# Weight sums for y by seven products: made by GpSimd alone, with longer DMA rows

## The chip, the cores and the metric

One NeuronCore of a Trainium2 chip runs the whole program. The metric is device time in microseconds, the median of several executions; lower is better. Engines in what follows: TensorE (PE), VectorE (DVE), ScalarE (ACT), GpSimd (POOL), and SyncE (SP), whose queue issues all DMAs of this kernel.

## The reference

Windowed attention over 8 x 8 heads of 576 positions with head dimension 64 (half of the heads look at the last 32 positions, half at every fourth of the last 128), and behind it a feed-forward layer with a PReLU over all 4608 tokens.

```
scores = scale * q @ k.T                    # (8, 8, 576, 576), masked to -1e9 outside the window
attn = exp(scores - max); attn = attn / (sum(attn) + 1e-9)
x = (attn @ v) as 4608 x 512
h = x @ w_in                                # w_in 512 x 2048
g = max(h, 0) + alpha * min(h, 0)
out = g @ w_out                             # w_out 2048 x 512
```

All of it in float32; a matrix operand is held as a high and a low float32r part, and a product is three passes (high-high, high-low, low-high).

## The kernel before, in words

The 4608 tokens are nine blocks of 512. Blocks 0 to 2 go through both layers in the plain form. Blocks 3 to 8 are done in pairs (t = 3, 5, 7), in `paired_stage` (L1155 onwards), which fills the span from about 348 us on. A pair (t, t+1) is done in two groups (grp 0, 1) of half the hidden units each. A group has a product stage for h and a stage for y.

- In the product stage h is made by seven matrix products instead of eight, on sums of quarter matrices. A unit of four hidden slices (four units, i = 0 to 3, to a group) takes products 1, 7, 6, 2, 5, 3, 4, each 12 matmuls in two blocks of 6 (`product`, L666); 3 and 4 are done within the next unit. Results lie in PSUM banks A, B, C. VectorE adds bank B or C to a staged copy (`add`, L715), which frees the bank for the next unit; ScalarE and VectorE then make the activation and its high and low parts (L722, L726, L730, L734).
- y of pair 3 is done plainly (`phase_y`, L930): 32 steps of 12 matmuls, in 4 output blocks c. y of pairs 5 and 7 is done by seven products too (`seven_y`, L1050), in 29 steps; there the finished banks are added to a partial sum in SBUF by `put` (L979), which frees them.
- The weights come from DRAM copies (wS for h, wO for y) made earlier, through a ring of ten places (`feed`, L614): each place is filled again when its weights have been used.
- y by seven products needs sums of the four quarters of w_out for each of eight sets i = 0 to 7 (NFP). They go into DRAM copy wY, and the ring reads them from there in pairs 5 and 7. `second_sum` (L1062) makes one set in three parts: `fetch` loads 1 MB of wO in four DMAs with rows of 512 B (L1074); `sums` does one addition of 128x1024 and four of 128x256 on VectorE (L1078, L1081); `parts` makes the high part on ScalarE (L1085) and the low part on VectorE (L1086) and stores both (L1088).
- The last 12 attention head pairs run within these stages: scores (L226, L250), maxima on VectorE (L283, L286), exponentials on ScalarE (L296), divisions and transpose on VectorE (L303 to L311), values (L326, L273). The next pair's k and q are loaded behind the scores, its v behind the values (L200, L201, L208).

Every engine runs its instructions in the order in which the code writes them; nothing reorders them. Work is put between the matmuls by hooks: a table from a step (of y) or a pair (unit, product) of the product stage to operations. `SUMS` (L1059) says at which step of which y stage a set's three parts stand: for (0, 0), that is pair 3 and grp 0, sets 1, 2, 3; for (0, 1) sets 4, 5; for (2, 0), pair 5 and grp 0, sets 6, 7. Set 0 is early: its loads are issued ahead of the first product stage, its `sums` stand in unit 0 behind product 6 and its `parts` behind product 5. Attention hooks of a step stand ahead of those of the sums. In `phase_y` a scoring stands at steps 2, 7, 12, 17, 22 in grp 0 and at 3, 8, 13 in grp 1; values follow eight steps later.

Buffers of the sets: `wy_spare` for set 0, and the ring's neighbours g1 to g4 (`gbuf`), two to a set, which also hold the staged copies of the product stage.

Of the kernel before, what the change touches and what calls it, by code (L numbers as in the profile page):

```python
# [8 lines left out]
F32 = mybir.dt.float32  # L9
F32R = mybir.dt.float32r  # L10
# [5 lines left out]
ALU = mybir.AluOpType  # L16

P = 128
# [7 lines left out]
HB = 9  # L26
# [5 lines left out]
NC = DM // P  # L32
NF = DFF // P
NSTD = 3
NFP = NF // 2
# [3 lines left out]
GP = 4  # L39
# [28 lines left out]
def tile_window_attention_prelu_ffn(  # L68
# [34 lines left out]
    marks = dram.tile([2 * NC, 1], F32, name="marks")  # L103
    wY = dram.tile([NFP, 4, P, 2, 2 * P], F32, name="wY")

# [71 lines left out]
    class Pair:  # L177
# [123 lines left out]
        def divisions(self):  # L301
            self.rs = rs = sml.tile([P, HB], F32, tag="rs", name=f"rs_{self.id}")
            nc.vector.tensor_scalar_add(rs, self.sm, 1e-9)  # L303
            nc.vector.reciprocal(out=rs, in_=rs)
            nc.vector.tensor_tensor(
                out=self.pr, in0=self.pr, in1=rs[:, :, None].broadcast_to([P, HB, BK]), op=ALU.mult)
# [217 lines left out]
    WBLOCK = {1: 0, 2: 1, 4: 2, 3: 3, 7: 4, 5: 5, 6: 6}  # L524
    YBLOCK = {6: 0, 7: 1, 3: 2, 5: 3}

# [50 lines left out]
    for t in range(NSTD, NTILE, 2):  # L577
        for grp in range(NFP // GP):
# [379 lines left out]
    def seven_y(t, grp, us, hooks):  # L958
# [72 lines left out]
        for n, (i, q) in enumerate(YSTEPS):  # L1031
# [11 lines left out]
            else:  # L1043
# [3 lines left out]
                for c in range(2):  # L1047
                    for k, (a, e) in enumerate(PASSES):
                        b = 2 * a + c if q in YBLOCK else 2 * c + a
# [9 lines left out]
    SUMS = {  # L1059
# [3 lines left out]
    }  # L1063

    def second_sum(i, rooms):


        room = {}

        def fetch():  # L1070
            room["x"], room["t"] = rooms()
# [4 lines left out]
        def sums():  # L1076
            x, t = (room[a].rearrange("p o c n -> p (o c n)") for a in "xt")
            nc.vector.tensor_tensor(out=t, in0=x, in1=t, op=ALU.add)  # L1078
            t = t.rearrange("p (q n) -> p q n", q=4)
# [3 lines left out]
        def parts():  # L1083
            x, t = (room[a].rearrange("p o c n -> p (o c n)") for a in "xt")
            nc.scalar.copy(out=x.bitcast(F32R), in_=t)  # L1085
            nc.vector.tensor_tensor(out=t.bitcast(F32R), in0=t, in1=x, op=ALU.subtract)  # L1086
            for a, w in enumerate((x, t)):
# [3 lines left out]
        return fetch, sums, parts  # L1091

    def second_sums(hooks, at):

        for i, *steps, k in SUMS.get(at, ()):
            ops = second_sum(i, lambda i=i, k=k: [gbuf([P, 2, NC, P], F32, f"wy{i}_{a}", k + a) for a in range(2)])
            for n, op in zip(steps, ops):
                hooks.setdefault(n, []).append(op)

# [56 lines left out]
    def paired_stage():  # L1156
# [4 lines left out]
        del cells["xB1"]  # L1161
        spare = const.tile([P, 2, 2, NC, P], F32, tag="xB1", name="wy_spare")
        early = second_sum(0, lambda: [spare[:, a] for a in range(2)])
        early[0]()
        late = []
        for t in range(NSTD, NTILE, 2):
            for grp in range(NFP // GP):
# [21 lines left out]
                if grp and t + 2 < NTILE:  # L1189
# [10 lines left out]
                second_sums(hooks, (t - NSTD, grp))  # L1200
                if seven:
# [49 lines left out]
    nc.vector.memset(pr0, 0.0)  # L1251
    nc.vector.memset(least, TOP_BIAS)
    pairs[0].load_qk()
    nc.sync.dma_start(out=pieces, in_=masks[:, 2 * NMASK:])
# [300 lines left out]
```

## Time and profile before

| | before |
|---|---|
| median of 3 runs | 876.75 us (875.34 to 880.34) |
| profiled execution, its own time | 878.21 us |
| its span | 876.1 us |
| TensorE busy | 839.7 us (96%) |
| VectorE busy | 623.8 us (71%) |
| ScalarE busy | 445.7 us (51%) |
| GpSimd busy | 47.0 us (5%), all of it before 320 us |
| DMA | 182.43 MB, 66.0% of the 16 engines' time |

A busy share is a mean over stages with different limits. What bounds a stretch is read from TensorE's waits there: a row of that view names the waiting engine and its instruction, then the engine and instruction that it waited for. Rows of the timeline carry start, duration, engine, line, operation, and in brackets the idle time ahead of the instruction and what ended it. A DMA row of SPq is the issue of a transfer on SyncE's queue and not the transfer itself.

### The profile page before, as it was taken

The page shows a single profiled execution, that of the slowest core. Times are in us where ns is not written, and L with a number is a line of the kernel's source. Part 1 is how long each engine was busy: PE and PEld are TensorE (multiplying, and loading weights), DVE is VectorE, ACT ScalarE, POOL GpSimd, SP SyncE. Part 2 cuts the span into 40 slices and gives each one's busy share as a digit, 9 for nine tenths or more (in the row PEclk, how much of TensorE's full clock was granted, in tenths as well). Part 3 has the DMA queues.
Part 4 walks back from the last instruction along what each step waited for, and adds up shares of the span by engine and source line. Part 5 has one row for each costly group of instructions (what it writes and reads, how often), then busy time and mean ns, then how long its engine had stood idle before and what let it go on. Part 6 is the DMA issues. An engine that isn't in the chain of part 4 may idle for free.

```text
span 876.1 us, 20220 instructions
## 1 busy us (share of the span) xinstructions
PE 839.7 (96%) x8094; PEld 684.3 (78%) x8094; DVE 623.8 (71%) x1071; ACT 445.7 (51%) x1226; POOL 47.0 (5%) x52
## 2 busy tenths in 40 slices
PE   7789999999999999699989998999899999999998
PEld 5567888888888888488778877888688888888886
DVE  5887766766676778477746787698649988843992
ACT  6785766424434444265435563566356536643650
POOL 0000000200514520000000000000000000000000
PEclk9999999999999999899999999999999999999999
DMA  7743344027899953778866688666965777666674
GB/s 254 255 160 120 137 165 150 28 92 218 276 288 315 301 193 116 253 220 237 283 223 194 172 258 284 213 195 209 327 212 180 203 258 215 193 196 192 194 207 145
DMA packets 134010, 182.43 MB, mean 208 GB/s; under 512 B 10014, under 2 KB 77726, under 8 KB 133918
## 3 DMA queue, kind: packets, MB, share of 16 engines
q1 hardware_dynamic: 133918, 181.15, 66.0%
q8 instruction: 64, 1.05, 0.5%
q14 instruction: 28, 0.23, 0.1%
HBM read 139.17 MB, written 41.94 MB: 207 GB/s over the span
## 4 chain that ended last, share of the span: by engine, by line
PE 83%; DMA 7%; DVE 5%; ACT 2%; SPq 2%; issue 2%; DVEq 0%; ACTq 0%
PE y L501 15%; PE h L453 15%; PE pA L666 14%; PE qA L1050 9%; PE pC L666 7%; PE y L930 6%; PE qC L1050 4%; PE pB L666 4%; PE o L326 3%; DMA q<-qT 2%; PE s L226 2%; PE qB L1050 2%; DMA wy<-wO 1%; DMA wy_spare<-wO 1%; PE s L250 1%
## 5 line engine op out<-in xcount | busy, mean ns | idle before, releaser
L453 PE MATMUL h<-x,w_dt.float32r 128*128 128x512 f32 x576 | 143.5, 399 | 0.9 <-ACT x L380 0.8
L501 PE MATMUL y<-g,w_dt.float32r 128*128 128x512 f32 x576 | 138.3, 389 | 0.0
L453 PEld LDWEIGHTS h<-x,w_dt.float32r 128*128 128x128 f32 x576 | 108.8, 191 | 24.5 <-ACT x L380 0.9
L501 PEld LDWEIGHTS y<-g,w_dt.float32r 128*128 128x128 f32 x576 | 108.0, 188 | 22.5
L296 ACT ACTIVATE pr<-pr,nm 128x64 f32<-128x64 f32 x216 | 72.3, 338 | 63.4 <-DVE nm L286 63.4
L479 ACT CAST g<-m 128x512 fp32r<-128x512 f32 x48 | 29.7, 619 | 74.8 <-DVE m L474 71.8
L666 PE MATMUL pA<-parts_w,ring_w 128*128 128x512 f32 x228 | 56.6, 390 | 0.0
L666 PE MATMUL pA<-parts_w,ring_xA 128*128 128x512 f32 x228 | 56.4, 390 | 0.0
L666 PEld LDWEIGHTS pA<-parts_w,ring_xA 128*128 128x128 f32 x228 | 42.7, 188 | 8.9
L666 PEld LDWEIGHTS pA<-parts_w,ring_w 128*128 128x128 f32 x228 | 42.7, 188 | 8.9
L806 DVE TENSOR_TENSOR gp<-stage,gp 128x512 fp32r<-128x512 f32 x64 | 42.8, 684 | 2.8 <-ACT gp L802 2.8
L484 DVE TENSOR_TENSOR g<-m,g 128x512 fp32r<-128x512 f32 x48 | 33.7, 701 | 15.5 <-ACT g L479 15.4
L1050 PE MATMUL qA<-gp,ring_w 128*128 128x512 f32 x162 | 40.9, 402 | 3.8 <-DVE py L979 3.8
L802 ACT CAST gp<-stage 128x512 fp32r<-128x512 f32 x64 | 37.5, 618 | 7.8 <-DVE stage L799 6.4
L473 DVE TENSOR_SCALAR m<-h,al 128x512 f32<-128x512 f32 x27 | 20.2, 749 | 29.7 <-PE h L453 29.7
L930 PE MATMUL y<-gp,ring_w 128*128 128x512 f32 x168 | 41.0, 396 | 0.0
L296 ACT ACTIVATION_READ_ACCUMULATOR pr<-pr,nm 128x1 f32 x216 | 40.9, 189 | 0.0
L1050 PEld LDWEIGHTS qA<-gp,ring_w 128*128 128x128 f32 x162 | 31.4, 195 | 10.9 <-DVE py L979 4.2
L666 PE MATMUL pC<-parts_w,ring_xA 128*128 128x512 f32 x114 | 29.6, 404 | 8.7 <-DVE stage L715 8.7
L722 ACT ACTIVATE n<-stage 128x512 f32<-128x512 f32 x44 | 27.9, 634 | 19.1 <-DVE stage L715 14.5
L930 PE MATMUL y<-gp,ring_xA 128*128 128x512 f32 x156 | 37.3, 393 | 0.0
L930 PEld LDWEIGHTS y<-gp,ring_w 128*128 128x128 f32 x168 | 31.5, 190 | 6.8
(181 smaller groups left out, 1604.3 us busy)
## 6 DMA issues: line engine op xcount, KB each, us to landing
ring_xA<-wS SPq DMA_DIRECT2D x67, 256.0 KB, 2.9
ring_w<-wS SPq DMA_DIRECT2D x66, 256.0 KB, 3.0
ring_g<-wS SPq DMA_DIRECT2D x35, 256.0 KB, 3.1
ring_w<-wO SPq DMA_DIRECT2D x34, 256.0 KB, 3.1
ring_xA<-wO SPq DMA_DIRECT2D x33, 256.0 KB, 3.0
wO<-w_dt.float32r SPq DMA_DIRECT2D x32, 256.0 KB, 4.5
wS<-wc SPq DMA_DIRECT2D x16, 512.0 KB, 4.5
wy<-wO SPq DMA_DIRECT2D x28, 256.0 KB, 5.0
```

Of the source, the lines that this page charges most:

```text
L296: nc.scalar.activation(out=self.pr[:, r, :], in_=self.ps[r // CUT0][:, r % CUT0, :] if self.onto else self.pr[:, r, :], func=AF.Exp, bias= ...
L326: nc.tensor.matmul(self.po[u][e * D:(e + 1) * D, a:z, :], lhsT=self.v[rows, i, :], rhs=self.pt[rows, a * BK + (BQ if i else 0):z * BK - (B ...
L453: nc.tensor.matmul(ms[t, f], lhsT=weight(0, a, f)[:, c * P:(c + 1) * P], rhs=half(t, c)[:, e, :], start=(c == 0 and n == 0), stop=(c == NC ...
L479: nc.scalar.copy(out=g[:, 0, :], in_=ms[t, f])
L484: nc.vector.tensor_tensor(out=g[:, 1, :], in0=ms.pop((t, f)), in1=g[:, 0, :].bitcast(F32), op=ALU.subtract)
L501: nc.tensor.matmul(ys[t][c], lhsT=weight(1, a, f)[:, c * P:(c + 1) * P], rhs=g[:, e, :], start=(first and n == 0), stop=(last and n == 2),)
L666: nc.tensor.matmul(to, lhsT=w[:, (2 * a + c) * P:(2 * a + c + 1) * P], rhs=part_of(name, e)[:, c * TT:(c + 1) * TT], start=start and c == ...
L722: nc.scalar.activation(out=self.m[n], in_=self.at(n), func=AF.Relu, scale=-1.0)
L802: nc.scalar.copy(out=self.pair(n)[:, 0], in_=self.whole(n))
L806: nc.vector.tensor_tensor(out=p[:, 1], in0=self.whole(n), in1=p[:, 0].bitcast(F32), op=ALU.subtract)
L930: nc.tensor.matmul(ys2[tt], lhsT=w[:, k * P:(k + 1) * P], rhs=g[:, e], start=j == 0 and n == 0, stop=j == GF - 1 and n == 2)
L1050: nc.tensor.matmul(named(to)[c], lhsT=w[:, b * P:(b + 1) * P], rhs=rhs[:, e], start=begins and k == 0, stop=i == GP - 1 and k == 2, skip_g ...
```

## The change

The sums of the eight sets are made by GpSimd alone: two additions of 128x512, four of 128x256, then a cast (high part) and a subtraction (low part) of 128x512 for each of two halves. GpSimd waits for the loads by itself. A set is loaded in two DMAs of 512 KB with rows of 2 KB and stored in two of 512 KB with one row of 4 KB for each partition; wY's layout changes with it, so that the ring reads its 64 wY units as two runs of 1 KB in place of one of 2 KB. A set now has two hooks, `start` and `store`. `SUMS` puts set 6 into the second y stage of pair 3 and leaves set 7 alone in pair 5. Set 1 takes the buffer of set 0. Set 0 starts behind product 5 of unit 0 and is stored behind product 6 of unit 2. Apart from this, the 1e-9 of the attention sums comes from a constant tile (tensor_tensor in place of tensor_scalar), and a memset fills that tile at the program's start.

```diff
-    wY = dram.tile([NFP, 4, P, 2, 2 * P], F32, name="wY")
+    wY = dram.tile([NFP, 2, P, 2, 2, 2, P], F32, name="wY")
+    tiny = const.tile([P, HB], F32, name="tiny")
...
-            nc.vector.tensor_scalar_add(rs, self.sm, 1e-9)
+            nc.vector.tensor_tensor(out=rs, in0=self.sm, in1=tiny, op=ALU.add)
...
-                        units.append(wY[grp * GP + i, YBLOCK[q]].rearrange("p a n -> p (a n)"))
+                        h, odd = YBLOCK[q]
+                        units.append(wY[grp * GP + i, h, :, :, odd].rearrange("p c a n -> p c (a n)"))
...
     SUMS = {
-        (0, 0): ((1, 3, 8, 11, 1), (2, 6, 13, 16, 3), (3, 16, 23, 26, 1)),
-        (0, 1): ((4, 3, 9, 12, 1), (5, 12, 19, 21, 3)),
-        (2, 0): ((6, 14, 19, 21, 1), (7, 14, 21, 23, 3)),
+        (0, 0): ((1, 1, 11, None), (2, 4, 17, 1), (3, 10, 23, 3)),
+        (0, 1): ((4, 3, 14, 1), (5, 8, 20, 3), (6, 18, 27, 1)),
+        (2, 0): ((7, 11, 23, 1),),
     }
...
-            for a, x in enumerate((room["x"], room["t"])):
-                for odd in range(2):
-                    nc.sync.dma_start(out=x[:, odd], in_=wO[i // GP, :, i % GP, :, odd, a].rearrange("c p n -> p c n"))
+            for h, x in enumerate(room):
+                nc.sync.dma_start(
+                    out=x.rearrange("p c o a n -> p c (o a n)"),
+                    in_=wO[i // GP, 2 * h:2 * h + 2, i % GP].rearrange("c p o a n -> p c (o a n)"))
...
-            nc.vector.tensor_tensor(out=t, in0=x, in1=t, op=ALU.add)
+            for x in room:
+                nc.gpsimd.tensor_tensor(out=x[:, :, :, 1], in0=x[:, :, :, 0], in1=x[:, :, :, 1], op=ALU.add)
...
-                nc.vector.tensor_tensor(out=t[:, out], in0=t[:, x], in1=t[:, y], op=op)
+                nc.gpsimd.tensor_tensor(out=t(out), in0=t(x), in1=t(y), op=op)
...
-            nc.scalar.copy(out=x.bitcast(F32R), in_=t)
-            nc.vector.tensor_tensor(out=t.bitcast(F32R), in0=t, in1=x, op=ALU.subtract)
+            for x in room:
+                nc.gpsimd.tensor_copy(out=x[:, :, :, 0].bitcast(F32R), in_=x[:, :, :, 1])
+                nc.gpsimd.tensor_tensor(
+                    out=x[:, :, :, 1].bitcast(F32R), in0=x[:, :, :, 1], in1=x[:, :, :, 0], op=ALU.subtract)
...
+        def store():
+            for h, x in enumerate(room):
                 nc.sync.dma_start(
-                    out=wY[i, :, :, a].rearrange("q p n -> p q n"), in_=w.rearrange("p (q n) -> p q n", q=4))
+                    out=wY[i, h].rearrange("p c o a n -> p (c o a n)"), in_=x.rearrange("p c o a n -> p (c o a n)"))
...
-        early[0]()
...
-                        ahead[0, 6], ahead[0, 5] = [early[1]], [early[2]]
+                        ahead[0, 5], ahead[2, 6] = [early[0]], [early[1]]
```

VectorE at the start of pair 3's first product stage (ob: results of block 2; wy_spare: set 0; stage, pB and pC: staged copy and banks of unit 0; n, gp: activation and its parts). Before:

```order
L511 COPY ob_7_1_4334<-y_8_1_3189 128x512
L511 COPY ob_7_3_4336<-y_8_3_3191 128x512
L1078 TENSOR_TENSOR wy_spare<-wy_spare 128x1024
L1081 TENSOR_TENSOR wy_spare<-wy_spare 128x256 x4
L715 TENSOR_TENSOR stage_4405<-pB_0_0_4397,stage_4374 128x512
L715 TENSOR_TENSOR stage_4417<-pC_0_0_4376,stage_4405 128x512
L1086 TENSOR_TENSOR wy_spare<-wy_spare 128x1024
```

VectorE at the same place in the changed kernel (L512 is the former L511, L717 the former L715, L728 the former L726):

```order
L512 COPY ob_7_1_4336<-y_8_1_3191 128x512
L512 COPY ob_7_3_4338<-y_8_3_3193 128x512
L717 TENSOR_TENSOR stage_4398<-pB_0_0_4390,stage_4372 128x512
L717 TENSOR_TENSOR stage_4410<-pC_0_0_4374,stage_4398 128x512
L728 SCALAR_TENSOR_TENSOR n_0_0_11_4408<-n_0_0_11_4408,bal,stage_4398 128x512
```

The six instructions of the sums of set 0 are gone from VectorE; the two additions from the banks follow the copies directly.

VectorE in pair 5's first y stage (nm: maxima of an attention head pair; wy: sets 6 and 7; py and qA: partial sum and bank of y). Before:

```order
L286 TENSOR_REDUCE nm_2_7293<-pr_78 128x4
L1078 TENSOR_TENSOR wy_1_7150<-wy_0_7149,wy_1_7150 128x1024
L1081 TENSOR_TENSOR wy_1_7150<-wy_1_7150 128x256 x4
L1086 TENSOR_TENSOR wy_1_7150<-wy_1_7150,wy_0_7149 128x1024
L1078 TENSOR_TENSOR wy_1_7156<-wy_0_7155,wy_1_7156 128x1024
L1081 TENSOR_TENSOR wy_1_7156<-wy_1_7156 128x256 x4
L979 TENSOR_TENSOR py_4881<-qA_5_0_6915,py_4881 128x512
```

VectorE at the same place in the changed kernel:

```order
L284 SCALAR_TENSOR_TENSOR pr_78<-s_2_0_7275,mask_sb 128x320
L287 TENSOR_REDUCE nm_2_7317<-pr_78 128x5
L284 SCALAR_TENSOR_TENSOR pr_78<-s_2_1_7276,mask_sb 128x256
L287 TENSOR_REDUCE nm_2_7317<-pr_78 128x4
L981 TENSOR_TENSOR py_4898<-qA_5_0_6937,py_4898 128x512
```

The addition to py (L981, the former L979) now follows the maxima; eleven instructions of sums that stood between are gone.

SyncE's queue at the start of pair 3's first y stage (k, q, v of the next head pairs, wy1 and wy2 the buffers of sets 1 and 2, ring the weights). Before:

```order
L200 DMA k_5_1_4754<-kT 128x576
L201 DMA q_5_1_4755<-qT 128x576
L614 DMA ring_g0_4357<-wO_83 128x512
L1074 DMA wy1_0_4779<-wO_83 128x4x128 x2
L1074 DMA wy1_1_4780<-wO_83 128x4x128 x2
L614 DMA ring_w2_1_3926<-wO_83 128x512
L1074 DMA wy2_0_4810<-wO_83 128x4x128 x2
L1074 DMA wy2_1_4811<-wO_83 128x4x128 x2
L614 DMA ring_w2_1_3926<-wO_83 128x512
L200 DMA k_5_2_4861<-kT 128x576
L201 DMA q_5_2_4862<-qT 128x576
```

SyncE's queue at the same place in the changed kernel (set 1 in wy_spare):

```order
L1075 DMA wy_spare_4363<-wO_83 128x2x512 x2
L201 DMA k_5_1_4769<-kT 128x576
L202 DMA q_5_1_4770<-qT 128x576
L616 DMA ring_g0_4359<-wO_83 128x512
L1075 DMA wy2_0_4800<-wO_83 128x2x512
L1075 DMA wy2_1_4801<-wO_83 128x2x512
L616 DMA ring_w2_1_3928<-wO_83 128x512 x2
L201 DMA k_5_2_4878<-kT 128x576
L202 DMA q_5_2_4879<-qT 128x576
```

Set 1's loads moved ahead of the first k and q, set 2's ahead of a ring load, and the eight issues became four.

## Rows read from the trace of the kernel before

**Rows 1.** TensorE's waits from 345 us: us in total, times, longest
```profile
PE pC L666 <- DVE stage L715: 8.7, 1, 8.7
PE s L250 <- DMA q<-qT: 4.0, 2, 3.0
PE qA L1050 <- DVE py L979: 3.8, 1, 3.8
PE o L273 <- DMA v<-vX: 2.7, 1, 2.7
```

**Rows 2.** Timeline around A: start and duration in us, engine, line, operation [idle before]
```profile
352.11 1.52 PE L666 MATMUL pB<-parts_w,ring_w 128*128 128x512 f32 x6
...
362.09 1.22 DVE L1078 TENSOR_TENSOR wy_spare<-wy_spare 128x1024 f32<-128x1024 f32 x1 [12.04 <-DMA wy_spare<-wO]
...
365.67 0.68 DVE L715 TENSOR_TENSOR stage<-pC,stage 128x512 f32<-128x512 f32 x1
...
366.41 2.93 PE L666 MATMUL pC<-parts_w,ring_xA 128*128 128x512 f32 x6 [8.70 <-DVE stage L715]
```

**Rows 3.** Timeline around B and C
```profile
407.63 2.65 SPq L1074 DMA_DIRECT2D wy<-wO  x4
...
412.28 0.42 SPq L201 DMA_DIRECT2D q<-qT  x1
...
419.11 1.04 PE L250 MATMUL s<-k,q 64*32 64x64 f32 x72 [1.07 <-DMA q<-qT]
...
440.63 0.97 PE L250 MATMUL s<-k,q 64*32 64x64 f32 x72 [2.97 <-DMA q<-qT]
```

**Rows 4.** Stretches: us, busy PE, PEld, DVE, ACT, POOL, granted clock, DMA share, GB/s
```profile
366.40:370.60 4.20, 4.19 (x11) 3.36 (x12) 3.21 (x5) 3.70 (x7) 0.00 (x0) 0.59 0.55 187
437.60:440.60 3.00, 0.06 (x1) 0.00 (x0) 0.00 (x0) 0.00 (x0) 0.00 (x0) 1.00 1.02 381
...
348.02:394.11 46.09, 37.39 (x158) 30.55 (x157) 28.34 (x43) 20.61 (x37) 0.00 (x0) 0.93 0.74 229
458.20:493.59 35.39, 35.39 (x158) 29.31 (x157) 23.37 (x35) 19.51 (x35) 0.00 (x0) 1.00 0.67 195
498.80:550.00 51.20, 48.52 (x652) 39.17 (x651) 40.44 (x73) 22.44 (x81) 0.00 (x0) 1.00 0.77 252
```

**Rows 5.** Timeline of VectorE around E
```profile
629.39 1.80 DVE L1081 TENSOR_TENSOR wy<-wy 128x256 f32<-128x256 f32 x4
...
631.12 1.28 DVE L979 TENSOR_TENSOR py<-qA,py 128x512 f32<-128x512 f32 x2
```

**Rows 6.** The chain that ended last: start and duration in us, what
```profile
366.41 4.58 PE pC L666 x12
...
377.79 2.72 PE pC L666 x12
...
441.61 5.90 PE y L930 x18
...
631.85 4.60 PE qA L1050 x12
```

**Rows 7.** GpSimd's two lines: duration min/median/max in ns, first and last start
```profile
L551 POOL TENSOR_TENSOR wsum_xA<-w_dt.float32r x12: 1288/1298/2207, 233.0 to 315.2; 128x512 f32<-128x512 f32 x12
...
L554 POOL TENSOR_TENSOR wsum_xA<-wsum_xA x24: 722/731/1057, 235.6 to 319.1; 128x256 f32<-128x256 f32 x24
```

**Rows 8.** DMA issues from 345 to 650 us: count, KB each, median us to landing
```profile
wy<-wO SPq DMA_DIRECT2D x28, 256.0 KB, 5.0
```

**Rows 9.** GpSimd and VectorE around 262 us, and VectorE's line L484 by duration
```profile
260.23 2.56 POOL L551 TENSOR_TENSOR wsum_xA<-w_dt.float32r 128x512 f32<-128x512 f32 x2 [21.36 <-DVE wc L564]
...
262.30 1.03 DVE L484 TENSOR_TENSOR g<-m,g 128x512 fp32r<-128x512 f32 x1 [0.76 <-ACT g L479]
...
L484 DVE TENSOR_TENSOR g<-m,g x48: 649/683/1030, 45.7 to 343.6; 128x512 fp32r<-128x512 f32 x48
```

**Rows 10.** VectorE's line L303 by duration in ns
```profile
L303 DVE TENSOR_SCALAR rs<-sums x32: 158/164/175, 12.5 to 657.9; 128x9 f32<-128x9 f32 x32
```

More of the change, by code (lines that the diff above doesn't have):

```diff
@@ L524, in tile_window_attention_prelu_ffn @@
     WBLOCK = {1: 0, 2: 1, 4: 2, 3: 3, 7: 4, 5: 5, 6: 6}
-    YBLOCK = {6: 0, 7: 1, 3: 2, 5: 3}
+    YBLOCK = {6: (0, 0), 7: (1, 0), 3: (0, 1), 5: (1, 1)}
     def save(f):
@@ L1048, in seven_y @@
                     for k, (a, e) in enumerate(PASSES):
-                        b = 2 * a + c if q in YBLOCK else 2 * c + a
+                        b = 2 * c + a
                         nc.tensor.matmul(
@@ L1059, in tile_window_attention_prelu_ffn @@
     SUMS = {
[3 rows of a table removed]
+        (0, 0): ((1, 1, 11, None), (2, 4, 17, 1), (3, 10, 23, 3)),
+        (0, 1): ((4, 3, 14, 1), (5, 8, 20, 3), (6, 18, 27, 1)),
+        (2, 0): ((7, 11, 23, 1),),
     }
     def second_sum(i, rooms):
-        room = {}
-        def fetch():
-            room["x"], room["t"] = rooms()
-            for a, x in enumerate((room["x"], room["t"])):
-                for odd in range(2):
-                    nc.sync.dma_start(out=x[:, odd], in_=wO[i // GP, :, i % GP, :, odd, a].rearrange("c p n -> p c n"))
@@ L1076, in sums @@
-        def sums():
-            x, t = (room[a].rearrange("p o c n -> p (o c n)") for a in "xt")
-            nc.vector.tensor_tensor(out=t, in0=x, in1=t, op=ALU.add)
-            t = t.rearrange("p (q n) -> p q n", q=4)
-            for out, x, y, op in ((3, 1, 3, ALU.add), (1, 0, 1, ALU.subtract), (0, 3, 0, ALU.subtract), (2, 2, 0, ALU.subtract)):
-                nc.vector.tensor_tensor(out=t[:, out], in0=t[:, x], in1=t[:, y], op=op)
-        def parts():
-            x, t = (room[a].rearrange("p o c n -> p (o c n)") for a in "xt")
-            nc.scalar.copy(out=x.bitcast(F32R), in_=t)
-            nc.vector.tensor_tensor(out=t.bitcast(F32R), in0=t, in1=x, op=ALU.subtract)
-            for a, w in enumerate((x, t)):
-                nc.sync.dma_start(
-                    out=wY[i, :, :, a].rearrange("q p n -> p q n"), in_=w.rearrange("p (q n) -> p q n", q=4))
@@ L1091, in second_sum, with start, t @@
[L1091 to L1098, printed above, removed]
+        room = []
+        def start():
+            room.extend(rooms())
+            for h, x in enumerate(room):
+                nc.sync.dma_start(
+                    out=x.rearrange("p c o a n -> p c (o a n)"),
+                    in_=wO[i // GP, 2 * h:2 * h + 2, i % GP].rearrange("c p o a n -> p c (o a n)"))
+            def t(q):
+                return room[q % 2][:, :, q // 2, 1]
+            for x in room:
+                nc.gpsimd.tensor_tensor(out=x[:, :, :, 1], in0=x[:, :, :, 0], in1=x[:, :, :, 1], op=ALU.add)
+            for out, x, y, op in ((3, 1, 3, ALU.add), (1, 0, 1, ALU.subtract), (0, 3, 0, ALU.subtract), (2, 2, 0, ALU.subtract)):
+                nc.gpsimd.tensor_tensor(out=t(out), in0=t(x), in1=t(y), op=op)
[3 more added lines that the diff above has]
+                    out=x[:, :, :, 1].bitcast(F32R), in0=x[:, :, :, 1], in1=x[:, :, :, 0], op=ALU.subtract)
@@ new lines, in store, with second_sums @@
+        def store():
+            for h, x in enumerate(room):
+                nc.sync.dma_start(
+                    out=wY[i, h].rearrange("p c o a n -> p (c o a n)"), in_=x.rearrange("p c o a n -> p (c o a n)"))
+        return start, store
+    def second_sums(hooks, at, spare):
+        for i, first, last, k in SUMS.get(at, ()):
+            start, store = second_sum(i, (lambda: spare) if k is None else (
+                lambda i=i, k=k: [gbuf([P, 2, 2, 2, P], F32, f"wy{i}_{a}", k + a) for a in range(2)]))
+            hooks.setdefault(first, []).append(start)
+            hooks.setdefault(last, []).append(store)
@@ L1161, in paired_stage @@
         del cells["xB1"]
-        spare = const.tile([P, 2, 2, NC, P], F32, tag="xB1", name="wy_spare")
-        early = second_sum(0, lambda: [spare[:, a] for a in range(2)])
-        early[0]()
+        both = const.tile([P, 2, 2, 2, 2, P], F32, tag="xB1", name="wy_spare")
+        spare = [both[:, h] for h in range(2)]
+        early = second_sum(0, lambda: spare)
         late = []
@@ L1199, in paired_stage @@
                                 hooks.setdefault(at + k, []).append(op)
-                second_sums(hooks, (t - NSTD, grp))
+                second_sums(hooks, (t - NSTD, grp), spare)
                 if seven:
@@ L1252, in tile_window_attention_prelu_ffn @@
     nc.vector.memset(least, TOP_BIAS)
+    nc.vector.memset(tiny, 1e-9)
     pairs[0].load_qk()
```

## The prediction, made before the changed kernel had run

> **What bounds the kernel now.** I read TensorE's waits first, then the timeline around each, then the windows for clock and DMA, and the chain for the price of a lowered clock. TensorE is the bound: the profiled execution takes 878.21 us, its span is 876.1, and in the paired stage (345 us to the end) TensorE idles five times, three times for a DMA and twice for VectorE [rows 1]. All five stand close to the weight sums for y.
>
> A, 8.70 us, up to 366.41. VectorE comes to the sums of set 0 and waits there 12.04 us for their loads. The additions L715 that free TensorE's banks stand behind the sums in VectorE's order, so pC starts when the second of them ends, at 365.67 + 0.68 [rows 2].
> B and C, 1.07 and 2.97 us: TensorE would score a head pair and q has not landed. Ahead of B, SyncE spent 2.65 us on issuing four loads of a set, and q's issue came only at 412.28 us [rows 3]; while TensorE waits in C the DMA engines are full, share 1.02 [rows 4].
> D, 2.7 us: the same for a v [rows 1].
> E, 3.8 us: in y by seven products the addition L979 that frees a bank of qA stands behind two sets of sums in VectorE's order; four of their additions take 1.80 us, and L979 runs at 631.12 us [rows 1, 5].
>
> The long waits cost more than their idle time. After A the granted clock is 0.59 for 4.2 us [rows 4], nearer the lower level (1.2 GHz) than 2.4 GHz, TensorE having been idle before. Twelve matmuls take 4.58 us there and 2.72 at full clock: 1.86 lost; after E 4.60, so 1.88; after C eighteen take 5.90 against 1.5 x 2.72 = 4.08, so 1.82 [rows 6]. For B and D I count nothing. So A is 10.56, E 5.65, C 4.79, B 1.07, D 2.7: together 24.8 us. A second reading of A agrees: the product stage that holds it takes 46.09 us, the same stage of the next group 35.39 [rows 4], which is 10.70 less.
>
> **The change part by part.**
> *The sums leave VectorE and ScalarE.* A sum that waits for its loads now stops GpSimd alone, which has nothing else to do in the paired stage. In VectorE's order the bank additions follow the copies of the stage before directly, and those of qA follow the maxima. What is late next at A: nothing that the next group's stage shows, whose TensorE is busy all its 35.39 us. At E three passes of 1.22 us (as in [rows 2]) and eight additions (2 x 1.80) leave VectorE ahead of L979: 631.12 - 7.3 = 623.8, before TensorE asks for it at 628.0 (631.85 less 3.8). So A and E go: 16.2 us.
>
> *GpSimd's time for a set, S.* Two additions of 128x512 (1.30 each), four of 128x256 (0.73), two casts and two subtractions of 128x512 (1.30) [rows 7]. No cast on GpSimd is in this trace; I bound it by GpSimd's addition of half its size, 0.73, and of its size, 1.30. S = 2.60 + 2.92 + 2c + 2.60 is 9.6 to 10.7 us; I take 10.2. If each instruction took the longest of its row (2.207 and 1.057, casts as additions), S = 6 x 2.207 + 4 x 1.057, less than 17.5 us.
>
> *Does a store hold up SyncE?* SyncE issues in order: behind a store that waits for GpSimd stand ring loads, k, q and v. In the first y stage sets 1 to 3 load at steps 1, 4, 10 and store at 11, 17, 23. The scoring of steps 12 and 22 would stand at 418.04 and 436.59 us without B and C (starts less waits, [rows 3]): 1.86 us a step. A load of a set lands in 5.0 us [rows 8]. Three sets one after another are done 5.0 + 3 x 10.2 = 35.6 us after step 1, set 3's store comes 22 steps or 40.9 us after it: 5 us of room; set 1 has 18.6 - 15.2 = 3.4. The second y stage now has three sets (4, 5, 6), the last store 24 steps after the first load; its steps 2 to 31 take (51.2 - 2.7) / 30 = 1.62 us each [rows 4], 38.8 in all, against 35.6: 3.2 us of room. A store that waits a little longer holds back ring loads, of which ten units are ahead. So nothing; without this cover each microsecond would cost one.
>
> *An interface in common?* VectorE's subtraction of two SBUF operands at 262.30 us took 1.03 us, its median being 0.683; it had begun within a GpSimd addition that ended at 262.79 [rows 9]. So 0.35 us for one that meets GpSimd, at most a whole addition, 1.30. In the y stages few such instructions run (one of 128x576 per head pair). In the product stage that now has set 0's sums beside it a unit of 9.5 us (seven products of half of 2.72) has seven, so about eight meet GpSimd: 2.8 us of VectorE time, 10.4 at most. In A VectorE's second L715 came some 11.4 us after the 354.3 at which it could have followed pB (352.11 + 1.52, and 0.68), and this cost 8.70; so 2.7 us of lateness are covered [rows 2]. TensorE loses 0.1 to 7.7 us; I take 1.0, near the measured 0.35 each.
> The Trainium skill speaks against the change here: "SBUF — State Buffer", section "Who interferes with whom", has a VectorE instruction with two SBUF inputs and a GpSimd instruction that reads SBUF exclude each other, each for its whole length. The trace agrees: 1.03 is 0.68 and most of what was left of the addition. By that rule the eight wait half of 1.30 each, an estimate of 5.2 us for VectorE and 2.5 for TensorE, and the sum would be 1.5 us more.
>
> *Loads and stores.* The bytes stay, 1 MB in and 1 MB out per set; a set has two load issues where it had four. In the first y stage loads come at steps 4 and 10 and the next k and q at 7 and 12; before, the loads of step 6 stood right ahead of the q of step 7 and those of step 16 ahead of the q of step 17. Queued from step 1 up to the q of step 7 are two sets, one k and q, three ring units: 3.5 MB, at 252 / 0.77 = 327 GB/s [rows 4] 10.7 us of 6 steps, 11.2 us. So q lands in time, B goes (1.07). At C the loads come six steps earlier, and the store that falls there stands behind k and q: 4.79 goes. D: set 5 loads four steps earlier: 2.7 goes. Against this the second y stage gets a third set, 2.1 MB or 6.4 us of DMA: 0.77 x 51.2 + 6.4 = 45.8 of 48.5 us, nearly full. A q or v may be late there, from nothing to a repeat of D; I take 1.5, about half. The ring's 64 wY loads go from rows of 2 KB to two runs of 1 KB, as the wO loads between them have them, which nobody waits for: nothing.
>
> *The added constant.* 32 additions of 128x9 change form, 0.164 us each before [rows 10]. They can gain no more than 5.2 us of VectorE time in all, and lose as much if the new form took twice as long; they lie beside queued matmuls. Nothing. One more memset stands ahead of the first load: nothing.
>
> Sum: 878.21 - 24.8 + 1.0 + 1.5 = 855.9. The median of the three runs, 876.75, is 1.46 under the profiled one: 854.5 us.
>
> **The rivals.**
> 1. *The DMA queues stay full.* The bytes don't fall, so B, C and D come back in other places, and A and E alone go: 876.75 - 16.2 = 860.5. For it: share 1.02 in C's wait. Against: the loads are spread ahead of k and q.
> 2. *Stores hold SyncE now and then.* At S = 14 set 3 is 5 + 42 - 40.9 = 6 us late and set 6 5 + 42 - 38.8 = 8. Behind the first is a v that is needed five steps (9.3 us) later and takes some 5 to land: 2 lost, and some 4 in ring loads behind the second, with one lowered clock (1.9): 854.5 + 8 = 862.5.
> 3. *It is slower.* The same mechanism, GpSimd the bound of both y stages. At S = 17.5 set 1 is late by 3.9 us, set 2 by 10.2, set 3 by 16.6, set 6 by 18.7; less what v's five steps and the ring's ten units cover, 12 us are lost, and 3.8 of clock after two idles: 16 of the 24.8. Each further microsecond of S costs three in each of two stages, so it decides from S of about 19; S = 20 gives 876.75 - 24.8 + 16 + 15 = 883. For it: VectorE can hold GpSimd up as GpSimd does VectorE. Against: even the longest rows make 17.5.
> 4. *It doesn't do at A what it says:* pC waited for a ring load that came at the same time. Then 10.56 stays, 865. Against: pC starts within 0.1 us of the end of L715.
>
> **How the numbers follow.** Forecast 0.60, rival 1 0.20, rival 2 0.08, rival 3 0.04, rival 4 0.04, and 0.04 that new waits eat the gain and the time stays within 0.5%. The forecast's own bounds: 852.0 with nothing given back, 854.5 + 6.7 = 861 with the 7.7 at A; the runs before lie 5 us apart, so 850 to 861. Rivals 1 and 2 take the upper end to 863. Left out are rivals 3, 4 and no change, 0.12. About 0.5% is what a measurement of this kernel can tell from no change. Faster 0.92, same 0.04, slower 0.04.
>
> **What would show it.** A: no wait of pC for VectorE above 2 us, and that product stage 35 to 38 us. E: no wait of qA. B to D: no wait for q or v above 1 us. S: the ten instructions of a set in 9.6 to 10.7 us where VectorE leaves them alone, and SyncE waits for GpSimd under 5 us in all. Wrong would be: VectorE's two-operand instructions in the first product stage above 1.3 us, SyncE held at the stores, or new waits for ring loads.

## The result and the profile after

The changed kernel takes 855.9 us against 876.6 us for the kernel before on the same chip: ratio 0.973, 95% interval 0.967 to 0.980. One of its four executions took 2124 us (and one of e8's, below, 1671), which nothing on record explains; the ratio compares the means of the other three (849.4, 855.3 and 856.5) and of the kernel before. Run again on another occasion it took 853.7 us against 878.6: 0.972 (0.967 to 0.976). The forecast was 854.5 us, 850 to 863. The execution that was profiled takes 855.32 us, its span 853.5.

TensorE's waits of the paired stage, which were five in [rows 1], are one (us in total, times, longest):

```profile
PE o L274 <- issue: 2.0, 1, 2.0
```

The stretches of [rows 4] after the change: the product stage beside set 0's sums, the first y stage, the next product stage, the two stretches around the one wait, and the rest up to the end (columns as in [rows 4]):

```profile
346.33:381.69 35.36, 35.36 (x157) 29.28 (x157) 26.73 (x37) 19.51 (x35) 12.73 (x10) 1.00 0.84 291
381.69:443.74 62.05, 60.06 (x985) 47.85 (x985) 32.41 (x71) 25.49 (x122) 28.79 (x30) 0.97 0.79 260
443.74:479.10 35.36, 35.36 (x157) 29.28 (x157) 23.37 (x35) 19.50 (x35) 0.00 (x0) 1.00 0.69 194
411.70:413.70 2.00, 0.02 (x3) 0.02 (x3) 0.00 (x0) 0.00 (x0) 2.00 (x2) 1.00 1.01 394
413.70:418.60 4.90, 4.90 (x36) 3.64 (x38) 3.94 (x8) 0.95 (x3) 4.59 (x6) 0.65 0.55 174
...
479.10:853.50 374.40, 370.58 (x2640) 304.18 (x2639) 269.74 (x424) 184.71 (x426) 46.80 (x40) 1.00 0.72 219
```

and the two of the kernel before that [rows 4] does not have, the first y stage and the rest:

```profile
394.11:458.20 64.09, 60.05 (x986) 47.91 (x985) 41.05 (x89) 28.39 (x125) 0.00 (x0) 0.97 0.80 247
493.59:876.10 382.51, 372.23 (x2640) 305.32 (x2639) 278.63 (x448) 188.48 (x430) 0.00 (x0) 0.99 0.70 215
```

The product stage of A falls from 46.09 to 35.36 us, which is what the stage without sums takes. The row of 46.09 starts a little early: in TensorE's chain the paired stage starts at 348.19 us before and at 346.33 after, so the stage took 45.92 and 10.56 are gained. The first y stage gains 2.04, the rest, with D and E in it, 8.11, the second product stage 0.03. Together 20.7 of the 22.9 us between the two profiled executions. Another 1.9 lie ahead of the paired stage, and 0.3 outside the span.

Ahead of the paired stage all kernels of this document run the same program, with or without the added constant, and yet in their profiles it starts anywhere from 344.1 to 349.7 us. So the 1.9 is no gain of the change, and where times lie close, the length of the paired stage in the profile says more. From its start in TensorE's chain to the end of the span it takes:

| kernel | paired stage, us |
|---|---|
| before | 527.9 |
| changed; changed, run again | 507.2; 507.0 |
| e1, e2, e9, e10 (edits of the kernel before) | 520.3, 528.5, 519.4, 505.5 |
| e3, e6, e7, e8 (edits of the changed kernel) | 516.3, 505.6, 504.2, 504.9 |
| e4; e4, run again | 503.3; 503.4 |

In the first y stage a new loss hides part of the gain. Its chain of waits (start, duration, what):

```profile
411.69 1.99 issue
...
414.10 4.54 PE y L932 x12
```

In the middle of one head pair's values, TensorE stands for 1.99 us on nothing that the profile shows, with the DMA share at 1.01; then the granted clock is 0.65, nearer 1.2 than 2.4 GHz, and twelve matmuls take 4.54 us where 2.72 is usual. That is 1.99 + 1.82 = 3.81 us. Without it this stage would have gained 5.85, and B and C were put at 1.07 + 4.79 = 5.86.

SyncE's queue there (start, duration, operation) has the store of set 2 behind the k and q of its step:

```profile
419.99 0.38 SPq L202 DMA_DIRECT2D q<-qT  x1
420.42 0.90 SPq L1093 DMA_DIRECT2D wY<-wy  x2
```

GpSimd's durations (min/median/max in ns, first and last start), and SyncE's waits for GpSimd:

```profile
L1083 POOL TENSOR_TENSOR wy<-wy x12: 1262/1288/1827, 402.6 to 599.6; 128x512 f32<-128x512 f32 x12
L1085 POOL TENSOR_TENSOR wy<-wy x12: 730/738/1714, 405.2 to 603.7; 128x256 f32<-128x256 f32 x12
L1087 POOL CAST wy<-wy x12: 611/616/1608, 408.9 to 606.4; 128x512 fp32r<-128x512 f32 x12
```
```profile
SPq L1093 <- POOL wy L1088: 9.1, 4, 4.6
SPq L1093 <- POOL wy_spare L1088: 4.0, 2, 2.5
```

With these rows a set comes to 2 x 1.29 + 4 x 0.74 + 2 x 0.616 + 2 x 1.29 = 9.4 us. In the trace sets 2 and 3, from first to last instruction, take 10.1 each; the others 10.2 to 15.2.

### The profile page after: what moved, and what is told of

Same layout as the page of the kernel before. It is cut to its first block, busy times and chain, and to the rows that moved or that the text cites. A ratio compares the mean times of both kernels' runs of the same rounds, so it can differ in the third digit from the quotient of the medians.

```text
span 853.5 us, 20230 instructions
## 1 busy us (share of the span) xinstructions
PE 834.7 (98%) x8094; PEld 681.1 (80%) x8094; DVE 604.6 (71%) x1024; ACT 438.1 (51%) x1218; POOL 135.3 (16%) x132
## 4 chain that ended last, share of the span: by engine, by line
PE 92%; DMA 3%; POOL 2%; issue 1%; DVE 1%; ACT 1%; SPq 0%; ACTq 0%; DVEq 0%
PE h L454 16%; PE y L502 15%; PE pA L668 15%; PE qA L1052 10%; PE y L932 9%; PE pC L668 8%; PE qC L1052 5%; PE pB L668 4%; PE o L327 3%; PE qB L1052 3%; PE s L227 2%; PE s L251 1%; PE o L274 1%; DMA wy<-wO 1%; POOL wy L1085 1%
## 5 line engine op out<-in xcount | busy, mean ns | idle before, releaser
L454 PE MATMUL h<-x,w_dt.float32r 128*128 128x512 f32 x576 | 140.8, 393 | 0.9 <-ACT x L381 0.8
L454 PEld LDWEIGHTS h<-x,w_dt.float32r 128*128 128x128 f32 x576 | 106.8, 188 | 23.7 <-ACT x L381 0.9
L474 DVE TENSOR_SCALAR m<-h,al 128x512 f32<-128x512 f32 x27 | 20.2, 749 | 29.8 <-PE h L454 29.8
L1052 PE MATMUL qA<-gp,ring_w 128*128 128x512 f32 x162 | 39.1, 390 | 0.0
L552 POOL TENSOR_TENSOR wsum_xB<-w_dt.float32r 128x512 f32<-128x512 f32 x4 | 5.1, 1296 | 211.0 <-PE h L454 164.1
L1083 POOL TENSOR_TENSOR wy<-wy 128x512 f32<-128x512 f32 x12 | 16.1, 1356 | 136.6 <-DVE pt L312 71.9
L1052 PE MATMUL qA<-gp,ring_xA 128*128 128x512 f32 x150 | 36.4, 390 | 0.0
```

The lines of the kernel that those rows point to most:

```text
L454: nc.tensor.matmul(ms[t, f], lhsT=weight(0, a, f)[:, c * P:(c + 1) * P], rhs=half(t, c)[:, e, :], start=(c == 0 and n == 0), stop=(c == NC ...
L474: nc.vector.tensor_scalar(out=m, in0=ps, scalar1=0.0, scalar2=al[:, f:f + 1], op0=ALU.min, op1=ALU.mult)
L1052: nc.tensor.matmul(named(to)[c], lhsT=w[:, b * P:(b + 1) * P], rhs=rhs[:, e], start=begins and k == 0, stop=i == GP - 1 and k == 2, skip_g ...
```

## The experiments

Ten more kernels ran, e1 to e10, and the changed kernel and e4 once more, each beside the kernel before on its chip (median there 877.9 us for e1 to e4, 879.7 for e6 to e9, 878.6 for e5, e10 and the two that ran again). Ratios stand to that.

### What A was: e1_set0_late

The kernel before, with set 0's sums and store two products later in VectorE's order.

```
-                        ahead[0, 6], ahead[0, 5] = [early[1]], [early[2]]
+                        ahead[2, 6], ahead[2, 5] = [early[1]], [early[2]]
```

> The kernel before, with one edit: the sums and parts of set 0 stand on VectorE and ScalarE two units later in the first product stage (unit 2, behind products 6 and 5), when their loads have long landed. Theory T (VectorE's order counts: a wait for a DMA ahead of bank additions holds TensorE): A alone goes, 8.7 us of idle time and 1.9 of lowered clock, so 866 us (864 to 868), and the stage of 46.1 us becomes 35.4 to 36. Rival U (VectorE's relief as such counts, 4.2 us for each of eight sets): VectorE does the same work, so within 2 us of before, 875 to 878.

Measured 867.18 us, ratio 0.989 (0.985 to 0.992). TensorE's waits:

```profile
PE s L250 <- DMA q<-qT: 4.2, 2, 3.2
PE qA L1050 <- DVE py L979: 3.8, 1, 3.8
PE o L273 <- DMA v<-vX: 3.0, 1, 3.0
```

pC's wait is gone and the other four stand as in [rows 1], 0.5 us longer in all; 10.7 us less by the medians (7 to 13 by the interval), where the prediction had A at 10.56. In the profile the stage takes 36.84 us, 9.1 less than before and 1.5 more than in the changed kernel: the sums still stand in VectorE's order. So A was the place of the sums in that order, and no other wait hung on it.

### GpSimd without anything else: e2_engine_alone, e9_engine_store, e10_store_steps

e2 is the kernel before with the sums, casts and subtractions on GpSimd; transfers and their places stay.

```
-            nc.vector.tensor_tensor(out=t, in0=x, in1=t, op=ALU.add)
+            nc.gpsimd.tensor_tensor(out=t, in0=x, in1=t, op=ALU.add)
...
-            nc.scalar.copy(out=x.bitcast(F32R), in_=t)
+            nc.gpsimd.tensor_copy(out=x.bitcast(F32R), in_=t)
```

> The kernel before, with the arithmetic of all eight sets on GpSimd and nothing else: loads, rows, stores and their steps as before. T: A and E go (10.6 and 5.7), B, C and D stay or change places (8.5 in all, since SyncE and the DMA queues see the same loads at the same steps), and stores wait for GpSimd, above all sets 6 and 7 whose loads come together: 861 us (858 to 866). U: the whole gain comes with the engine, 855 to 857.

Measured 875.32 us, ratio 0.998 (0.994 to 1.0005): both theories missed. TensorE's waits, and SyncE's for GpSimd:

```profile
PE pC L666 <- DMA ring_xA<-wS: 7.1, 1, 7.1
PE s L250 <- DMA q<-qT: 5.7, 2, 4.6
PE o L273 <- DMA v<-vX: 4.6, 1, 4.6
```
```profile
SPq L1088 <- POOL wy L1085: 13.5, 5, 5.2
SPq L1088 <- POOL wy L1086: 11.3, 6, 2.4
SPq L1088 <- POOL wy_spare L1085: 9.7, 1, 9.7
```

E is gone, as forecast. A is not: the wait has moved to another engine's order. SyncE reaches set 0's store, waits 9.7 us for GpSimd (which starts only at 358.92 us, when the loads have landed), and the ring load that pC needs stands behind it. The waits for q and v are longer than before.

e9 moves set 0's store alone, to the place it has in the changed kernel:

```
-                        ahead[0, 6], ahead[0, 5] = [early[1]], [early[2]]
+                        ahead[0, 6], ahead[2, 6] = [early[1]], [early[2]]
```

> e2_engine_alone (875.3 us), with one edit more: set 0's store is issued at the place where the changed kernel has it, two products later, instead of in front of the ring loads that pC waited for. Theory T (in e2 the wait at A only moved from VectorE to SyncE, which stood at this store): the 7.1 us wait of pC for a ring load goes and with it one lowered clock, 875.3 - 9 = 866 (863 to 869); waits for q and v stay. Rival U (the ring load was late because the DMA queues were full): the wait stays, 872 to 876.

Measured 867.45 us, ratio 0.988 (0.983 to 0.993). The 7.1 us wait is gone, so it was the store ahead of the ring load. What stays:

```profile
PE s L250 <- DMA q<-qT: 5.7, 2, 4.2
PE o L273 <- DMA v<-vX: 4.5, 1, 4.5
PE o_a L273 <- issue: 1.5, 1, 1.5
```

SyncE's queue in e9 ahead of C and ahead of D, each with TensorE's late instruction:

```profile
415.77 3.23 SPq L1088 DMA_DIRECT2D wY<-wy  x2
419.06 3.06 SPq L1074 DMA_DIRECT2D wy<-wO  x4
...
423.50 0.42 SPq L201 DMA_DIRECT2D q<-qT  x1
```
```profile
429.47 1.32 PE L250 MATMUL s<-k,q 64*32 64x64 f32 x72 [4.19 <-DMA q<-qT]
```
```profile
509.85 2.87 SPq L1088 DMA_DIRECT2D wY<-wy  x2
512.81 2.81 SPq L1074 DMA_DIRECT2D wy<-wO  x4
...
520.38 0.34 SPq L208 DMA_DIRECT2D v<-vX  x1
```
```profile
526.18 1.60 PE L273 MATMUL o<-pt,v 32*64 32x32 f32 x84 [4.48 <-DMA v<-vX]
```

Both times a set's store and the next set's loads stand together, 2 MB of transfers, ahead of the q or v that comes late. SyncE also stands still ahead of both stores, 2.2 and 3.9 us, until GpSimd has the set ready. In e10 four stores, and no load, are issued one to three steps later (the casts are written next to the sums for it, which leaves GpSimd's order as it was):

```
-        (0, 0): ((1, 3, 8, 11, 1), (2, 6, 13, 16, 3), (3, 16, 23, 26, 1)),
-        (0, 1): ((4, 3, 9, 12, 1), (5, 12, 19, 21, 3)),
-        (2, 0): ((6, 14, 19, 21, 1), (7, 14, 21, 23, 3)),
+        (0, 0): ((1, 3, 8, 11, 1), (2, 6, 13, 17, 3), (3, 16, 23, 26, 1)),
+        (0, 1): ((4, 3, 9, 14, 1), (5, 12, 19, 21, 3)),
+        (2, 0): ((6, 14, 19, 23, 1), (7, 14, 21, 26, 3)),
```

> e9_engine_store (867.45 us) with four stores issued later: set 2's one step later (17 instead of 16, so behind the k and q of that step and no longer in one lump with the loads of set 3), set 4's two steps later (14 instead of 12, where set 5 loads), sets 6 and 7 two and three steps later. Loads stay as in the kernel before: its steps, four issues, rows of 512 bytes; the stores keep rows of 1 KB. Theory P (q and v were late because a store and the next set's loads stood together ahead of them on SyncE): no wait for q or v above 1.6 us, 851 to 856. Rival W (the stores' rows of 4 KB were needed): waits for q or v stay, 860 to 868.

Measured 853.97 us, ratio 0.971 (0.967 to 0.975). Its SyncE queue at C, and its waits:

```profile
412.95 2.87 SPq L1074 DMA_DIRECT2D wy<-wO  x4
...
418.46 0.42 SPq L201 DMA_DIRECT2D q<-qT  x1
418.97 0.93 SPq L1089 DMA_DIRECT2D wY<-wy  x2
```
```profile
PE s L250 <- DMA q<-qT: 1.0, 2, 0.5
PE pB L666 <- DMA ring_w<-wS: 0.9, 1, 0.9
```

13.5 us under e9 by the medians, some 14 by the paired stage. C falls from 4.19 to 0.42 us and D from 4.48 to nothing; with the two lowered clocks behind them, at the 1.82 and 1.86 of [rows 6], that is 11.9. The rest isn't tied to the moved stores: B, ahead of which none of them stands, happens to be 1.0 shorter (0.53), a wait of 1.5 without a releaser has gone, and 0.9 for a ring load has come. The loads still have the steps, the four issues and the 512-byte rows of the kernel before.

What helps at C is when q is issued, and not how fast it comes: 418.46 instead of 423.50 us, 5.0 earlier, while in the chain it takes 6.48 us to land against 5.84 in e9. SyncE's wait for GpSimd (2.2) and the store's issue (3.23) had stood ahead of it. The move takes the wait, the issue and the store's transfer out of q's way together; what each is worth alone was not run.

### The rows and the number of transfers: e4_old_places, e6_four_short, e8_four_long

e4 is the changed kernel with the loads at the steps of the kernel before (and the stores where e10 has them):

```
-        (0, 0): ((1, 1, 11, None), (2, 4, 17, 1), (3, 10, 23, 3)),
-        (0, 1): ((4, 3, 14, 1), (5, 8, 20, 3), (6, 18, 27, 1)),
-        (2, 0): ((7, 11, 23, 1),),
+        (0, 0): ((1, 3, 11, None), (2, 6, 17, 1), (3, 16, 26, 3)),
+        (0, 1): ((4, 3, 14, 1), (5, 12, 21, 3)),
+        (2, 0): ((6, 14, 23, 1), (7, 14, 26, 3)),
```

> The changed kernel, with the loads of sets 1 to 7 at the steps of before (3, 6, 16; 3, 12; 14, 14) and stores late enough for GpSimd (11, 17, 26; 14, 21; 23, 26). GpSimd and the long rows are kept. T: what kept q and v late were the places of the loads, so B, C and D come back at least in part, in all 4 to 9 us: 862 us (859 to 866). U, or if the longer rows are what freed the queues: 854 to 857.

Measured 851.49 us, ratio 0.971 (0.968 to 0.974), below the ranges of both theories, and TensorE waits nowhere in the paired stage. So the new steps of the loads, on which my account of B to D rested, are not what freed q and v. That left the rows, the issues or the stores. e6 and e8 are e4 with four loads per set, in e6 with rows cut to 512 bytes, in e8 with rows of 2 KB. e6:

```
+                for c in range(2):
                     nc.sync.dma_start(
-                        out=x.rearrange("p c o a n -> p c (o a n)"),
-                        in_=wO[i // GP, 2 * h:2 * h + 2, i % GP].rearrange("c p o a n -> p c (o a n)"))
+                        out=x.rearrange("p o a c n -> p (o a) c n")[:, :, c],
+                        in_=wO[i // GP, 2 * h + c, i % GP].rearrange("p o a n -> p (o a) n"))
```

(the buffer is laid out as p o a c n for it, and the ring reads rows of 2 KB). e8:

```
+                for c in range(2):
                     nc.sync.dma_start(
-                        out=x.rearrange("p c o a n -> p c (o a n)"),
-                        in_=wO[i // GP, 2 * h:2 * h + 2, i % GP].rearrange("c p o a n -> p c (o a n)"))
+                        out=x[:, c].rearrange("p o a n -> p (o a n)"),
+                        in_=wO[i // GP, 2 * h + c, i % GP].rearrange("p o a n -> p (o a n)"))
```

> e4_old_places (851.5 us, no wait in the paired stage) with each set loaded by four transfers of 256 KB whose rows are cut to 512 bytes, as in the kernel before; steps, engine and stores stay those of e4. Theory R, it was the short rows that made q and v late: the issues take 2 us and more for four as in [rows 3], waits for q or v come back and the time is 857 to 861 (851.5 + up to 8.5). Rival I, it was the number of issues on SyncE: the same 857 to 861 here, but in e8_four_long too. Rival S, it was neither (the stores' long rows or the engine alone did it): 850.5 to 853 here and in e8_four_long, no wait for q or v.

> e4_old_places with each set loaded by four transfers of 256 KB in rows of 2 KB. Theory R (short rows): 850.5 to 853, no wait for q or v, since the rows stay long. Rival I (number of issues): 857 to 861, with waits for q or v above 1 us. Rival S (neither): 850.5 to 853.

Measured 853.1 us, ratio 0.972 (0.966 to 0.978), for e6 and 853.73 us, 0.972 (0.967 to 0.977), for e8. e8 waits 0.5 us for a v and 0.7 without a releaser. e6 waits for q, at the places of B and C:

```profile
PE s L251 <- DMA q<-qT: 2.2, 2, 1.6
```
```profile
405.06 0.99 PE L251 MATMUL s<-k,q 64*32 64x64 f32 x72 [1.65 <-DMA q<-qT]
...
424.15 0.97 PE L251 MATMUL s<-k,q 64*32 64x64 f32 x72 [0.58 <-DMA q<-qT]
```

By the times neither the rows nor the number of issues makes a difference that these runs can tell. So neither was what made C and D long, as rival S had it. Its own reasons, long rows of the stores or the engine alone, fall too: e9 has the engine and waits, e10 has stores with rows of 1 KB and waits 0.5 us at most. For C and D it is the stores' place.

B is another matter. Rival S had no wait for q in e6, and there is one. B stands in every profile whose loads have rows of 512 bytes (0.5 to 1.7 us: before, e1, e2, e9, e10, e6) and, of those with 2 KB, only in e3 (0.7) and e5 (0.3); e8 has the four issues too, and no wait there. The paired stage agrees: e6 takes 2.2 us more than e4, which is its two waits. So the short rows seem to cost 1 to 2 us, most of it at B, in single profiles; the times are too wide to show that. (e6 also lets the ring read wY in rows of 2 KB, so it sends 127,867 packets in all, not many more than the 123,771 of e8.)

### The transfers without GpSimd: e3_dma_alone

The changed kernel with the additions and subtractions on VectorE and the casts on ScalarE, three steps ahead of each store (set 0's in unit 1, behind product 5):

```
+            hooks.setdefault(last - 3, []).append(make)
...
-                        ahead[0, 5], ahead[2, 6] = [early[0]], [early[1]]
+                        ahead[0, 5], ahead[1, 5], ahead[2, 6] = [early[0]], [early[1]], [early[2]]
```

> The changed kernel, with the arithmetic back on VectorE and ScalarE, three steps ahead of each store (set 0: unit 1, behind product 5); loads, rows and stores as in the changed kernel. T: A stays away since the loads have landed by then; B, C and D stay away since the loads stand where the change puts them; VectorE gets 4.2 us a set back in nine-tenths full y stages, which costs nothing but where a bank addition stands right behind: 859 us (856 to 864). U: the gain goes with VectorE's relief, 870 to 876.

Measured 864.66 us, ratio 0.986 (0.982 to 0.989), just over the range of T, whose y stages "nine-tenths full" no row shows (VectorE was busy 41.05 of 64.09 us in the first). TensorE's longest waits:

```profile
PE o L274 <- issue: 2.0, 1, 2.0
PE s L251 <- DVE ob L955: 1.8, 2, 1.5
...
PE pB L668 <- DVE stage L717: 1.3, 1, 1.3
```

All five waits of [rows 1] have gone or shrunk below 1 us without GpSimd. In their place come many small waits for VectorE, which still has the sums. With the sums at these places GpSimd is worth the rest, 9 us by the times and by the paired stage, some 11 by the ratios; other places on VectorE were not run. The wait of 2.0 us without a releaser is here too.

### How far the cover reaches: e5_longer_sets

The changed kernel with each cast carried out nine times over.

```
-                nc.gpsimd.tensor_copy(out=x[:, :, :, 0].bitcast(F32R), in_=x[:, :, :, 1])
+                for _ in range(9):
+                    nc.gpsimd.tensor_copy(out=x[:, :, :, 0].bitcast(F32R), in_=x[:, :, :, 1])
```

> The changed kernel with GpSimd's two casts of each set carried out nine times instead of once: 16 more casts of 0.616 us, so a set takes some 10.1 + 9.9 = 20 us, which is the case that the prediction's third rival priced. Theory R3 (a store that waits holds SyncE and each microsecond beyond the cover costs one): 875 to 888, slower than or near the kernel before. Rival H (the ring loads and v's that stand behind have more cover than I gave them, as when SyncE waited 34 us in e2_engine_alone and TensorE lost 10 more than with e9's store): 860 to 870.

Measured 922.05 us, ratio 1.049 (1.044 to 1.054), far over both. A set takes 21 to 27 us. The waits:

```profile
PE o L274 <- DMA v<-vX: 27.4, 3, 12.0
PE pA L668 <- ACT stage L901: 20.2, 1, 20.2
PE pA L668 <- DMA ring_xA<-wS: 8.6, 1, 8.6
```
```profile
SPq L1094 <- POOL wy L1089: 87.7, 11, 11.4
```
```profile
ACT stage L901 <- DMA wY<-wy: 24.4, 1, 24.4
```

The v's and q's behind held stores are the third rival's mechanism. Two waits are not in its price. Set 0's store holds a ring load in the product stage (8.6). And ScalarE's copy L901, by which the product stage behind the second y stage frees a bank, writes a buffer that set 6's store must have left (20.2). Taken off with a lowered clock of 1.86 for each, 922.05 - 8.6 - 20.2 - 3.7 = 889.5. The rival's own working, 883 at S = 20 and 6 more per microsecond, gives 889 at 21, the time of the quicker sets, but 902 at 23.1, the mean of sets 1 to 6. So its mechanism is shown, and its price, at one value of S, is right to some 12 us.

### The wait that the profile does not explain: e7_set3_later, after_again, e4_again

e7 loads set 3 four steps later and stores it two steps later:

```
-        (0, 0): ((1, 1, 11, None), (2, 4, 17, 1), (3, 10, 23, 3)),
+        (0, 0): ((1, 1, 11, None), (2, 4, 17, 1), (3, 14, 25, 3)),
```

> The changed kernel with set 3 loaded at step 14 and stored at step 25 of the first y stage instead of 10 and 23. Theory T (the 2.0 us in which TensorE waits for nothing at 413.7 us, and the lowered clock behind it, come from DMA queues filled by the loads of that set): the DMA share around there falls below 0.95, the stall goes, 855.9 - 3.8 = 852.1 (851 to 854). Rival U (the stall has nothing to do with the loads): it stays at the same matmuls, 855 to 857.

Measured 851.85 us, ratio 0.970 (0.966 to 0.975). The time is T's, but the reason is not. The wait of 2.0 us is gone (one of 0.7 us is left, at 425 us) while the DMA engines are full all the same (columns as in [rows 4]):

```profile
412.00:416.00 4.00, 4.00 (x85) 3.14 (x86) 3.18 (x9) 0.91 (x3) 1.70 (x2) 1.00 1.04 361
```

Full DMA engines alone therefore do not stop TensorE. In the changed kernel one transfer of the instruction queue falls within 411.0 to 411.7 us, where the wait begins (queue, kind: packets, MB, share):

```profile
q8 instruction: 1, 0.02, 8.4%
```

8.4% of 16 engines for 0.7 us is 0.94 us for that packet. In all three profiles with this wait (the changed kernel's two and e3's) such a packet stands right ahead of it, with the DMA engines 94% busy or more with other transfers. But such packets come in other places without a wait, in e4 at 414.5 us with the engines as full, and the profile does not say whose instructions they are. That TensorE waited for its own is only a guess; the cause stays open. Nor is such a wait new: the kernel before has three at head pairs' values, all ahead of the paired stage:

```profile
PE o L326 <- issue: 5.4, 3, 2.2
```

The changed kernel and e4 then ran once more together, unchanged.

> The changed kernel once more, beside e4_old_places on the same chip. Theory T (the stall for no shown reason in the first y stage is a property of its program): 854 to 857, with the stall. Rival U (the stall comes and goes from one execution to the next): 849 to 856, profile without the stall or with it elsewhere.

> e4_old_places once more beside the changed kernel on the same chip. If the older places of the loads are better, its time is 3 to 4 us below the changed kernel's (851 to 852.5 against 855 to 857); if the difference was the spread between executions, the two intervals overlap.

Measured 853.72 us, ratio 0.972 (0.967 to 0.976), for the changed kernel and 851.05 us, 0.968 (0.964 to 0.972), for e4. The changed kernel's profile has the wait at the same matmuls, shorter:

```profile
PE o L274 <- issue: 1.4, 1, 1.4
```

Theory T held in that the wait is a property of its program; the time is 0.3 us under T's range. Neither profile of e4 has the wait. The intervals of the times overlap. The paired stage settles more: 507.2 and 507.0 us for the changed kernel, 503.3 and 503.4 for e4, so e4 gains 3.7 us there, about what the wait and its clock cost in the two profiles, 3.81 and 3.25 (1.42 + 1.83).

## Why the prediction was right, and where its steps were not

**A, 10.56: right.** The stage gained 10.56, and e1 gained 10.7 by the medians, 9.1 in the stage, by the order alone. But "the sums leave VectorE ... so A and E go" left out a condition. e2 moves the sums and keeps set 0's store in place, and A's wait comes back as a ring load's. The change also moves that store; the step for SyncE looked at the stores in the y stages and not at this one.

**E, 5.65: right.** No wait of qA is left, in e2 either.

**B to D, 8.56: right in size, wrong in cause.** They went. For all three the text gave the reason that the loads come at other steps, and for C one more, that a store now stands behind k and q. e4 has the old load steps and no wait, so the new steps were not needed; whether they would have been enough with the old stores was not run. For C the second reason was enough, and for D, where the text did not give it, too: e10 has the old loads altogether, and what it moves on SyncE is stores alone. What made C and D was a store in one lump with the next set's loads, with SyncE waiting at it, ahead of a q or v. (That is shown with the sums on GpSimd; in the kernel before itself the stores were not moved.) B goes with the rows of the loads, as far as the profiles of e6 and e8 show, and the text had that term right without this reason. Rival 1, that full queues bring the waits back, did not come: the changed kernel waits for no q and no v.

**GpSimd's time.** Taken at 10.2; 10.1 undisturbed, within 9.6 to 10.7. The cast, 0.616 us, lies below my lower bound of 0.73. Beside a busy VectorE a set takes up to 15.2.

**SyncE held at stores: under 5 us forecast, 13.1 measured.** By the prediction's own signs this was one of being wrong, and VectorE's 1.77 us in the first product stage (below) was another. The times came out all the same: TensorE lost nothing that shows by either, the cover being where it was put. In e5, past the cover, two places were missing.

**Given back, 2.5 forecast.** The contention with GpSimd took 2.6 us more of VectorE in that product stage: 26.73 us in 37 records, against 24.10 before in as many, 28.34 less the 4.24 of the sums. The prediction's 2.8 was near, and TensorE lost none of the 1.0 there. The page "SBUF — State Buffer" of the Trainium skill ("Who interferes with whom") has a VectorE instruction with two SBUF inputs and a GpSimd instruction that reads SBUF exclude each other, and the trace agrees: L736 took up to 1.77 us for a median of 0.684, and GpSimd's additions up to 1.83 for 1.29. The estimates from it, 5.2 us for VectorE and 2.5 for TensorE, did not come: VectorE lost half of the one, and its lateness was covered. The 1.5 for a full second y stage did not come either, since the rest of the kernel gained 8.11 of 8.35. What was given back is the 3.81 that nobody had in the sum. So the total was right to 1.4 us partly by luck: 2.5 forecast as lost were not lost, 3.81 were lost elsewhere, and 2.2 of the measured gain lie outside the paired stage, where nothing but the constant changed.

## What to carry to other kernels

Moving work to an idle engine moves the wait to whoever stands next in an order: here SyncE, at the store of the result, with everybody's loads behind it. Look for each store that must wait, and put it behind the loads that are needed first and apart from the next block of loads. Four store steps were worth 13.5 us here, of which 11.9 can be traced to them. The rows of the loads were worth 1 to 2 us at most, and their number nothing that could be measured. And where two kernels lie a few microseconds apart, compare the stage that was changed and not the whole time: here the unchanged part alone differs by 5.5 us from profile to profile.

## What was unexpected on the chip

A GpSimd cast of 128x512 from float32 to fp32r takes 0.616 us, half of an addition of that size (1.29). VectorE and GpSimd hold each other up both ways, casts too: one took 1.61 us beside a VectorE instruction with two SBUF operands that was running when it began. TensorE can stand for 2 us in the middle of a run of matmuls for no reason in the profile, twice at the same matmuls of the changed kernel, and lose nearly as much again to the lowered clock (1.99 us and 1.82).
